# Moving four weight conversions from the second feed-forward layer into the first, in a fused attention and two-layer kernel

## The chip, the cores and the metric

The kernel runs on one core of one Trainium2 chip. The metric is the device time of one execution in microseconds. The kernel before was run three times on the clock alone, and once more with the profiler; the rows below come from that profiled execution.

## The reference

```python
def _attn_ref(q, k, v):                      # (2, 8, 576, 64), rotary positions
    q_rot, k_rot = (rotate(q), rotate(k))
    scores = np.matmul(q_rot, k_rot.transpose(0, 1, 3, 2)) / np.sqrt(D)
    attn = np.exp(scores - np.max(scores, axis=-1, keepdims=True))
    attn = attn / (np.sum(attn, axis=-1, keepdims=True) + 1e-09)
    return np.matmul(attn, v)

def _moe_ref(x, w_in, w_out):                # x (1152, 512), w_in (512, 2048), w_out (2048, 512)
    h = x @ w_in
    g = np.where(h > 0.0, h, np.exp(np.minimum(h, 0.0)) - 1.0)
    return g @ w_out

def _moe2_ref(x, w_in, w_out):               # same shapes, weights of its own
    h = x @ w_in
    return (h * np.tanh(softplus(h))) @ w_out
```

The attention result, laid out as 1152 tokens by 512 features, goes through the first layer and then through the second. The four weight arrays arrive as 64-bit floats.

## The kernel before

Every product is made from high and low parts of its operands: a value is kept as a rounded high part and the remainder, and three matrix products (high with high, low with high, high with low) are added up. XH and XL are the two parts of a layer's input, wi and wo followed by h or l those of its weights (a digit 0 or 1 tells even from odd groups, which have buffers of their own), g and ge those of the activated hidden values.

**The steps.** The 2048 hidden features are cut into 16 slices of 128, four slices make a group (GF = 4), and the tokens into two halves b of 576. A step is one slice for one half: 32 steps for the first layer, n = 0 to 31, and 32 for the second, n = 32 to 63; `half` in the code is 32. In each step TensorE runs `g1_mm` (24 matmuls, L183) into one of two PSUM buffers ps_s. In the first layer ScalarE (ACT) and VectorE (DVE) then make the ELU: L214, L215 and L216 on ACT, L217 and L218 on DVE (L218 is the last reader of ps_s), L223 on ACT (the high part) and L227 on DVE (the low part). When a group is complete for a half, four second products are due (`g2_first`, 24 matmuls, L619), one in each of the next four steps; DVE adds their result to Y at L629. For the last group of a half, L632 adds, L633 on ACT makes XH of the second layer and L634 on DVE makes XL. In the second layer L575 and L576 on ACT read ps_s, L577, L590 and L597 on DVE and L583, L589 and L596 on ACT follow, and `g2_second` (L648) multiplies with the output weights into ps_h. The steps 32 to 35 use the first four slices of the second layer, 36 to 39 the next four.

**The weight jobs.** One slice of one weight array is one job, 64 in all, in the order of the list `jobs`. A job loads the raw 64-bit words (SP queue, three buffers raw) and turns them into a 32-bit float wu (two buffers) and then into its two parts. It is opened with L96 on GpSimd (POOL) and goes on in four parts: a is L100, b is L104 and c is L108, all on DVE; d is L122 on ACT (the high part) and then L123 on POOL (the low part). `weight_part` does one part of the oldest open job, and two jobs are open at a time. Jobs 40 to 43 are the output weights wo0 of the second layer's first group, which its first `g2_second` needs.

**What sets the order.** In the first layer every engine's instructions stand in the order in which the code writes them. In a step from 4 to 30 there are three parts ahead of the ELU's first half and one part between its two halves, so each step does one job. From step 31 on, each step ends with one whole job, step 36 with two. In the second layer only ACT keeps the written order; a scheduler orders the others.

Of the kernel before, what the change touches and what calls it, by code (L numbers as in the profile page):

```python
# [27 lines left out]
def kernel(  # L28
# [22 lines left out]
    GF = 4  # L51
# [98 lines left out]
    def weight_part():  # L150
        while len(running) < 2 and opened[0] < len(jobs):
            open_job()
        if running:
            advance(0)

    def weight_job():
        n = min(njob[0] + 1, len(jobs))
        while njob[0] < n:
            weight_part()
# [15 lines left out]
    def g1_mm(m, f, b):  # L175
        c = m * NF + f
        hi, lo = WI[c]
        o = ps_s()
        k = 0
        for cc in range(NC):  # L180
            for w, x in ((hi, XH), (hi, XL), (lo, XH)):
                for j in range(2):
                    nc.tensor.matmul(  # L183
                        o[:, j, :HS], lhsT=w[:, cc, :], rhs=x[:, b, cc, j * HS:j * HS + HS],
                        start=(k == 0), stop=(k == 3 * NC - 1),
                    )
                k += 1
        return o
# [22 lines left out]
    def elu(m, f, b, o):  # L211
        h = o[:, :, :HS]
        t, g = tmp("ta"), tmp("tb")
        nc.scalar.activation(out=v2(g), in_=h, func=AF.Relu, scale=-1.0)  # L214
        nc.scalar.activation(out=t, in_=g, func=AF.Exp, scale=-1.0)  # L215
        nc.scalar.activation(out=g, in_=g, func=AF.Tanh, scale=-0.5)  # L216
        nc.vector.scalar_tensor_tensor(out=g, in0=t, scalar=1.0, in1=g, op0=ALU.add, op1=ALU.mult)  # L217
        nc.vector.tensor_tensor(out=v2(g), in0=v2(g), in1=h, op=ALU.max)  # L218
        return m, f, b, g

    def elu_hi(m, f, b, g):
        gh, gl = galloc(m, f, b)
        nc.scalar.activation(out=gh, in_=g, func=AF.Copy)  # L223
        return g, gh, gl

    def elu_lo(g, gh, gl):
        nc.vector.tensor_tensor(out=gl, in0=g, in1=plain(gh), op=ALU.subtract)  # L227
# [329 lines left out]
    def moe(mp, early):  # L557
# [15 lines left out]
        def mish_a(n, m, f, b, o):  # L573
            t, s = tmp("ta"), tmp("tb")
            nc.scalar.activation(out=v2(t), in_=o[:, :, :HS], func=AF.Tanh, scale=0.5)  # L575
            nc.scalar.activation(out=v2(s), in_=o[:, :, :HS], func=AF.Silu)  # L576
            nc.vector.scalar_tensor_tensor(out=s, in0=t, scalar=-3.0, in1=s, op0=ALU.add, op1=ALU.mult)  # L577
            mst[n] = (m, f, b, t, s)

        def mish_b(ns):  # L580
            for n in ns:
                t = mst[n][3]
                nc.scalar.activation(out=t, in_=t, func=AF.Ln, scale=-NEAR_HALF, bias=half_col)  # L583

        def mish_c(ns):
            nc.scalar.preload_act_table_set("silu_and_others")
            for n in ns:
                m, f, b, t, s = mst[n]
                nc.scalar.activation(out=t, in_=t, func=AF.Tanh, scale=-1.0)  # L589
                nc.vector.scalar_tensor_tensor(out=s, in0=t, scalar=1.0, in1=s, op0=ALU.add, op1=ALU.mult)  # L590

        def mish_d(ns):
            for n in ns:
                m, f, b, t, s = mst.pop(n)
                gh, gl = galloc(m, f, b)
                nc.scalar.activation(out=gh, in_=s, func=AF.Copy, scale=-0.25)  # L596
                nc.vector.scalar_tensor_tensor(  # L597
                    out=gl, in0=s, scalar=-0.25, in1=plain(gh), op0=ALU.mult, op1=ALU.subtract
                )
                seam(m, f, b)  # L600
# [60 lines left out]
        blocks[-4:] = [(1, g, b) for g in range(NG - 2, NG) for b in range(NB)]  # L661
        g1_seq = [(m, g * GF + fi, b) for m, g, b in blocks for fi in range(GF)]
        half = len(g1_seq) // 2
        D1, D2, LATE, XJ = 1, 4, (3, 4, 5, 7), 4
        pend = []

        def run_g2(it):
            if it[0] == 0:
                g2_first(*it[1])
            else:  # L670
                g2_second(*it[1])
# [6 lines left out]
        def step(n, late):  # L678
            m, f, b = g1_seq[n]
            o = early.pop(n) if n in early else g1_mm(m, f, b)  # L680
            if late:
                mish_c(late)
            done, late = late, []
            if m == 0:
                for _ in range(3 if GF <= n < half - 1 else 0):
                    weight_part()
                if o is not None:
                    o = elu(m, f, b, o)
                if GF <= n < half - 1:
                    weight_part()  # L690
                if o is not None:
                    o = elu_hi(*o)
            else:
                mish_a(n, m, f, b, o)
                mish_d(done)
            if f % GF == GF - 1:
                g = f // GF
                if m == 0:
                    pend.extend((n + (D1 if n < half - 1 else LATE[e]), (0, (g, b, e))) for e in range(NC))
                else:  # L700
                    pend.extend((n + D2, (1, (g, t))) for t in TB[b])
            if n in batches:
                late = batches[n]
                mish_b(late)
            cnt = 2 if len(pend) > 5 or pend and pend[0][1][0] == 0 and n in (half - 2, half + 6) else 1
            while pend and cnt and pend[0][0] <= n:
                run_g2(pend.pop(0)[1])
                cnt -= 1
            if m == 0:
                if o is not None:  # L710
                    elu_lo(*o)
            for _ in range(0 if n < half - 1 else 1 + (n == half + XJ)):
                weight_job()
            return late

# [9 lines left out]
        with tc.manual_schedule():  # L725
            while njob[0] < 2 * GF:
                weight_job()
            for n in range(half):
                step(n, [])
        with tc.manual_schedule(engines=MANUAL):  # L730
            late = []
            for n in range(half, 2 * half):
                if n == half + 7:
                    psum("ps_h")
                    s_more[0] = g_pool[0]
                    s_count[0] = 0
                late = step(n, late)
            mish_c(late)
            mish_d(late)
            while pend:  # L740
                run_g2(pend.pop(0)[1])
# [19 lines left out]
    with tc.tile_pool(name="mp", bufs=1, reuse_waits="tile") as mp:  # L761
        moe(mp, early)
# [54 lines left out]
```

## Time and profile before

| what | value |
|---|---|
| runs on the clock alone | 607.88, 608.4, 611.34 us; median 608.4 us |
| the profiled execution's own time | 612.44 us |
| its span, first to last instruction | 610.7 us |
| TensorE busy | 581.3 us (95%) |
| VectorE, ScalarE, GpSimd busy | 451.3, 372.4, 255.0 us |
| mean granted TensorE clock | 0.974 of full speed |

Busy shares are means over the attention (to about 200 us), the first layer (to about 385 us) and the second. What a stage is worth is read from its own stretch and from what its engines wait for.

### The profile page before, as it was taken

To read this page: it belongs to the slowest core of one execution; us is meant where nothing else is said; L and a number is where in the kernel's file an instruction comes from. 1 tells how busy PE (TensorE), PEld (TensorE's weight loads), DVE (VectorE), ACT (ScalarE), POOL (GpSimd) and SP (SyncE) were. 2 spreads that over 40 slices of the span, in tenths; PEclk is the share of its full clock that TensorE was granted. 3 is DMA by queue.
4 is the path that set the end of the run, shared out by engine and by line. 5 is a ranking of instruction groups with operands and counts; after the bars stand their busy time and mean duration, and the time that the engine had idled before them with its cause. 6 is when DMAs were issued, how large, how long until landed. Compare 5 with 4: busy or idle time off the path is not lost.

```text
span 610.7 us, 10253 instructions
## 1 busy us (share of the span) xinstructions
PE 581.3 (95%) x3794; PEld 503.7 (82%) x3794; DVE 451.3 (74%) x681; ACT 372.4 (61%) x637; POOL 255.0 (42%) x226
## 2 busy tenths in 40 slices
PE   6799999988899999999999999997899999999997
PEld 6676656655568999999999999996699998989985
DVE  5888998999972676677777778798588677674552
ACT  3357676765874665654545555793867868378660
POOL 5596685667780133232232332355243433532000
PEclk8779999998999999999999999999799999999999
DMA  6483577844530122232221322233332432300022
GB/s 215 128 234 115 115 195 196 240 105 126 163 99 0 35 101 75 70 104 70 84 91 69 104 70 75 68 124 99 103 90 83 138 87 70 121 18 1 17 85 89
DMA packets 43921, 62.17 MB, mean 102 GB/s; under 512 B 13920, under 2 KB 32096, under 8 KB 43104
## 3 DMA queue, kind: packets, MB, share of 16 engines
q1 hardware_dynamic: 43872, 61.52, 34.0%
q8 instruction: 30, 0.49, 0.3%
q14 instruction: 19, 0.16, 0.1%
HBM read 46.20 MB, written 2.36 MB: 80 GB/s over the span
## 4 chain that ended last, share of the span: by engine, by line
PE 36%; issue 28%; DVE 19%; POOL 13%; ACT 1%; DMA 1%; SPq 0%; POOLq 0%; ACTq 0%; DVEq 0%
PE ps_h L648 16%; PE ps_s L183 13%; DVE P L397 6%; DVE mn L373 5%; POOL wu L96 4%; PE ps_s L366 3%; POOL wi1l L123 3%; POOL wo0l L123 2%; PE psT L405 2%; PE psA L426 2%; POOL wo1l L123 2%; POOL wi0l L123 2%; DVE rc L390 2%; DVE wu L104 2%; DVE wu L100 1%
## 5 line engine op out<-in xcount | busy, mean ns | idle before, releaser
L380 ACT ACTIVATE P<-ps_s,mn 128x576 f32<-128x576 f32 x72 | 53.4, 741 | 39.1 <-DVE mn L373 30.7
L123 POOL TENSOR_TENSOR wi1l<-wu,wi1h 128x512 fp32r<-128x512 f32 x16 | 25.2, 1577 | 91.7 <-ACT wi1h L122 91.7
L373 DVE TENSOR_REDUCE mn<-ps_s 128x1 f32<-128x576 f32 x72 | 53.9, 748 | 11.4 <-PE ps_s L366 11.3
L405 PE MATMUL psT<-idn,P 128*128 128x128 f32 (+1 forms) x360 | 55.0, 286 | 6.5 <-DVE P L397 3.2
L417 ACT ACTIVATE pt<-psT 128x640 f32<-128x640 f32 x64 | 44.9, 702 | 23.9 <-PE psT L405 23.2
L100 DVE TENSOR_SCALAR wu<-wu 128x512 int32<-128x512 int32 x64 | 32.9, 514 | 34.0 <-POOL wu L96 34.0
L183 PE MATMUL ps_s<-XH,wi1h 128*128 128x288 f32 x256 | 55.1, 296 | 1.5 <-ACT tb L576 1.5
L183 PE MATMUL ps_s<-XH,wi0h 128*128 128x288 f32 x256 | 55.2, 297 | 0.9 <-DVE tb L218 0.8
L397 DVE TENSOR_SCALAR P<-P,rc 128x576 f32<-128x576 f32 x56 | 54.3, 970 | 1.0
L183 PE MATMUL ps_s<-XH,wi1l 128*128 128x288 f32 x256 | 54.8, 295 | 0.0
L183 PE MATMUL ps_s<-XL,wi1h 128*128 128x288 f32 x256 | 54.8, 295 | 0.0
L183 PE MATMUL ps_s<-XL,wi0h 128*128 128x288 f32 x256 | 54.7, 295 | 0.0
L183 PE MATMUL ps_s<-XH,wi0l 128*128 128x288 f32 x256 | 54.6, 295 | 0.0
L426 PE MATMUL psA<-pt,v_t 128*64 128x256 f32 (+1 forms) x320 | 54.5, 433 | 0.0
L104 DVE SCALAR_TENSOR_TENSOR wu<-raw,wu 128x512 int32<-128x512 int32 x64 | 51.1, 798 | 1.9
L108 DVE SCALAR_TENSOR_TENSOR wu<-raw,wu 128x512 int32<-128x512 int32 x64 | 50.6, 790 | 1.7
L405 PEld LDWEIGHTS psT<-idn,P 128*128 128x128 f32 (+1 forms) x360 | 40.7, 140 | 12.1 <-issue 3.7
L123 POOL TENSOR_TENSOR wo1l<-wu,wo1h 128x512 fp32r<-128x512 f32 x16 | 24.1, 1508 | 62.5 <-ACT wo1h L122 62.5
L96 POOL TENSOR_SCALAR wu<-raw 128x512 f32<-128x512 f32 x64 | 47.5, 743 | 5.1
L217 DVE SCALAR_TENSOR_TENSOR tb<-ta,tb 128x576 f32<-128x576 f32 x30 | 22.7, 758 | 34.1 <-ACT tb L216 33.8
L214 ACT ACTIVATE tb<-ps_s 128x576 f32<-128x576 f32 x30 | 19.6, 652 | 43.3 <-PE ps_s L183 43.3
L575 ACT ACTIVATE ta<-ps_s 128x576 f32<-128x576 f32 x32 | 20.6, 644 | 40.3 <-PE ps_s L183 40.3
(138 smaller groups left out, 1546.7 us busy)
## 6 DMA issues: line engine op xcount, KB each, us to landing
raw<-in_w_in_dram SPq DMA_DIRECT2D x32, 512.0 KB, 3.7
raw<-in_w_out_dram SPq DMA_DIRECT2D x32, 512.0 KB, 3.3
qk_t<-in_qk_dram SPq DMA_DIRECT2D x6, 1152.0 KB, 6.9
qa<-qh SPq DMA_DIRECT2D x28, 144.0 KB, 5.6
v_t<-in_vp_dram SPq DMA_DIRECT2D x8, 320.0 KB, 3.6
out_dram<-Y SPq DMA_DIRECT2D x9, 256.0 KB, 2.0
ka<-kh SPq DMA_DIRECT2D x14, 144.0 KB, 6.1
ka<-kl SPq DMA_DIRECT2D x14, 144.0 KB, 5.8
```

The costliest lines, as they stand in the source:

```text
L96: nc.gpsimd.tensor_scalar(out=u, in0=high.bitcast(F32), scalar1=REBASE, scalar2=0.0, op0=ALU.mult, op1=ALU.add)
L104: nc.vector.scalar_tensor_tensor(out=ui, in0=high, scalar=-0x80000000, in1=ui, op0=ALU.bitwise_and, op1=ALU.bitwise_or)
L108: nc.vector.scalar_tensor_tensor(out=ui, in0=low, scalar=29, in1=ui, op0=ALU.logical_shift_right, op1=ALU.bitwise_or)
L123: nc.gpsimd.tensor_tensor(out=lo, in0=u, in1=plain(hi), op=ALU.subtract)
L183: nc.tensor.matmul(o[:, j, :HS], lhsT=w[:, cc, :], rhs=x[:, b, cc, j * HS:j * HS + HS], start=(k == 0), stop=(k == 3 * NC - 1),)
L373: nc.vector.tensor_reduce(out=m, in_=psS[u][:, :, :HS], axis=AX.XY, op=ALU.min)
L380: nc.scalar.activation(out=P.rearrange("p (j n) -> p j n", j=2), in_=psS.pop(u)[:, :, :HS], func=AF.Exp, scale=-1.0, bias=mn_t.pop(u), acc ...
L397: eng.tensor_scalar(out=P, in0=P, scalar1=r, scalar2=None, op0=ALU.mult)
L405: nc.tensor.transpose(tv[:w, c, :], P[:, c * 128:c * 128 + w], idn)
L417: nc.scalar.activation(out=o, in_=tv, func=AF.Copy)
L426: nc.tensor.matmul(o[64 * h:64 * h + 64, :n], lhsT=v_t[p][:, c, 64 * h:64 * h + 64], rhs=pt_t[p, g][:, h, c, :], start=(c == 0), stop=(c = ...
L648: nc.tensor.matmul(o, lhsT=l, rhs=w, start=(k == 0), stop=(k == 3 * GF - 1))
```

## The change

```diff
-        D1, D2, LATE, XJ = 1, 4, (3, 4, 5, 7), 4
+        D1, D2, LATE = 1, 4, (3, 4, 5, 7)
+        AHEAD = half - 1 - 4 * GF
@@ in step(n, late)
-                for _ in range(3 if GF <= n < half - 1 else 0):
+                for _ in range((4 if n >= AHEAD else 3) if GF <= n < half - 1 else 0):
                     weight_part()
                 if o is not None:
                     o = elu(m, f, b, o)
@@ at the end of step
-            for _ in range(0 if n < half - 1 else 1 + (n == half + XJ)):
+            for _ in range(0 if n < half - 1 or half + 4 <= n < half + 7 else 1):
                 weight_job()
```

AHEAD is 15. In steps 15 to 30 five parts are done in place of four: four ahead of the ELU's first half and one between the halves. The 16 extra parts are four jobs, so job 39 instead of 35 is the next to finish when step 31 begins. In the second layer steps 36 to 38 finish no job, where steps 36, 37 and 38 finished two, one and one before; from step 39 on the two kernels are in phase again. No instruction is added or taken away.

A job takes four parts and a step now does five, so the place of the parts turns with a period of four steps (15 to 18, 19 to 22, 23 to 26, 27 to 30): `abcd|a`, `bcda|b`, `cdab|c`, `dabc|d`, the bar standing for the ELU's first half.

On ScalarE, the end of step 14, step 15 and most of step 16 (L122 is part d). Before:

```order
L223 ACTIVATE g<-tb 128x576
L214 ACTIVATE tb<-ps_s 128x576
L215 ACTIVATE ta<-tb 128x576
L216 ACTIVATE tb<-tb 128x576
L122 ACTIVATE wi0h<-wu 128x512
L223 ACTIVATE g<-tb 128x576
```

and with the change:

```order
L223 ACTIVATE g<-tb 128x576
L122 ACTIVATE wi0h<-wu 128x512
L214 ACTIVATE tb<-ps_s 128x576
L215 ACTIVATE ta<-tb 128x576
L216 ACTIVATE tb<-tb 128x576
L223 ACTIVATE g<-tb 128x576
L122 ACTIVATE wo0h<-wu 128x512
```

Part d stood behind L216 and now stands in front of L214; in every fourth step (`dabc|d`) a second one stands behind L216 as well.

On VectorE, from the last instruction of step 15 to the end of step 16. Before:

```order
L227 TENSOR_TENSOR g<-tb,g 128x576
L100 TENSOR_SCALAR wu<-wu 128x512
L104 SCALAR_TENSOR_TENSOR wu<-raw,wu 128x512
L108 SCALAR_TENSOR_TENSOR wu<-raw,wu 128x512
L217 SCALAR_TENSOR_TENSOR tb<-ta,tb 128x576
L218 TENSOR_TENSOR tb<-tb,ps_s 128x576
L629 TENSOR_TENSOR Y<-Y,ps_g 128x576
```

and with the change:

```order
L227 TENSOR_TENSOR g<-tb,g 128x576
L104 SCALAR_TENSOR_TENSOR wu<-raw,wu 128x512
L108 SCALAR_TENSOR_TENSOR wu<-raw,wu 128x512
L100 TENSOR_SCALAR wu<-wu 128x512
L217 SCALAR_TENSOR_TENSOR tb<-ta,tb 128x576
L218 TENSOR_TENSOR tb<-tb,ps_s 128x576
L104 SCALAR_TENSOR_TENSOR wu<-raw,wu 128x512
L629 TENSOR_TENSOR Y<-Y,ps_g 128x576
```

Part c, L108, which the L122 in front of this step's L214 waits for, still comes behind the L227 of the step before, and a fourth part stands between L218 and L629.

On ScalarE, from the last conversion of step 36 to step 38 (L575 and L576 read ps_s of a step; L633 writes XH). Before:

```order
L633 ACTIVATE XH<-Y 128x576
L122 ACTIVATE wo0h<-wu 128x512 x2
L575 ACTIVATE ta<-ps_s 128x576
L576 ACTIVATE tb<-ps_s 128x576
L122 ACTIVATE wo0h<-wu 128x512
L575 ACTIVATE ta<-ps_s 128x576
L576 ACTIVATE tb<-ps_s 128x576
L633 ACTIVATE XH<-Y 128x576
L122 ACTIVATE wo0h<-wu 128x512
```

and with the change:

```order
L633 ACTIVATE XH<-Y 128x576
L575 ACTIVATE ta<-ps_s 128x576
L576 ACTIVATE tb<-ps_s 128x576
L575 ACTIVATE ta<-ps_s 128x576
L576 ACTIVATE tb<-ps_s 128x576
L633 ACTIVATE XH<-Y 128x576
```

All four conversions to wo0h have left this place; they now stand between steps 31 and 36, where conversions to wi1h and wi0h stood, as many as before.

## Rows read from the trace of the kernel before

**Rows 1.** Busy time by stretch: length, then each engine's us, clock, DMA share, GB/s.

```profile
290.00:380.00 90.00, 90.00 (x680) 90.00 (x679) 68.56 (x102) 47.01 (x73) 27.85 (x28) 1.00 0.27 83
...
417.67:436.13 18.46, 12.04 (x50) 9.24 (x50) 13.05 (x17) 10.08 (x16) 8.26 (x8) 0.82 0.41 128
436.13:582.00 145.87, 145.87 (x876) 132.59 (x875) 99.99 (x146) 104.15 (x161) 48.14 (x38) 1.00 0.23 68
```

**Rows 2.** Timeline of TensorE, steps 38 to 41: start, us, instruction, [idle before it <-releaser].

```profile
417.25 0.42 PE L619 MATMUL ps_g<-g,wo1l 128*128 128x288 f32 x2
419.16 0.54 PE L183 MATMUL ps_s<-XH,wi1h 128*128 128x288 f32 x2 [1.49 <-ACT tb L576]
...
429.26 1.22 PE L648 MATMUL ps_h<-wo0h,g 128*128 128x512 f32 x2 [4.00 <-ACT wo0h L122]
...
436.13 0.43 PE L183 MATMUL ps_s<-XH,wi0h 128*128 128x288 f32 x2
...
439.31 0.63 PE L648 MATMUL ps_h<-wo0h,g 128*128 128x512 f32 x2
...
444.91 0.42 PE L183 MATMUL ps_s<-XH,wi0h 128*128 128x288 f32 x2
```

**Rows 3.** Timelines of DVE and ACT: part c, its part d and what follows.

```profile
421.86 0.69 DVE L108 SCALAR_TENSOR_TENSOR wu<-raw,wu 128x512 int32<-128x512 int32 x1
...
422.59 0.63 ACT L122 ACTIVATE wo0h<-wu 128x512 fp32r<-128x512 f32 x1 [3.48 <-DVE wu L108]
423.12 0.64 ACT L575 ACTIVATE ta<-ps_s 128x576 f32<-128x576 f32 x1
```

**Rows 4.** Timeline of step 25 from the end of its L183 matmuls, all engines.

```profile
340.35 0.69 PE L619 MATMUL ps_g<-g,wo0h 128*128 128x288 f32 x4
340.55 0.65 ACT L214 ACTIVATE tb<-ps_s 128x576 f32<-128x576 f32 x1 [1.94 <-PE ps_s L183]
341.24 0.69 ACT L215 ACTIVATE ta<-tb 128x576 f32<-128x576 f32 x1
341.95 0.69 ACT L216 ACTIVATE tb<-tb 128x576 f32<-128x576 f32 x1
342.67 0.76 DVE L217 SCALAR_TENSOR_TENSOR tb<-ta,tb 128x576 f32<-128x576 f32 x1 [1.35 <-ACT tb L216]
343.53 0.75 DVE L218 TENSOR_TENSOR tb<-tb,ps_s 128x576 f32<-128x576 f32 x1
344.20 0.75 DVE L629 TENSOR_TENSOR Y<-Y,ps_g 128x576 f32<-128x576 f32 x1
345.04 0.89 DVE L227 TENSOR_TENSOR g<-tb,g 128x576 fp32r<-128x576 f32 x1
345.86 0.42 DVE L100 TENSOR_SCALAR wu<-wu 128x512 int32<-128x512 int32 x1
346.31 0.69 DVE L104 SCALAR_TENSOR_TENSOR wu<-raw,wu 128x512 int32<-128x512 int32 x1
346.95 0.65 ACT L214 ACTIVATE tb<-ps_s 128x576 f32<-128x576 f32 x1 [1.94 <-PE ps_s L183]
347.03 0.69 DVE L108 SCALAR_TENSOR_TENSOR wu<-raw,wu 128x512 int32<-128x512 int32 x1
```

**Rows 5.** Timelines of DVE, ACT and PE: the last XL, and the start of step 32.

```profile
379.68 0.75 DVE L632 TENSOR_TENSOR Y<-Y,ps_g 128x576 f32<-128x576 f32 x1
...
380.46 0.68 ACT L633 ACTIVATE XH<-Y 128x576 fp32r<-128x576 f32 x1 [2.85 <-DVE Y L632]
...
381.18 0.76 DVE L634 TENSOR_TENSOR XL<-Y,XH 128x576 fp32r<-128x576 f32 x1 [0.75 <-ACT XH L633]
...
381.86 0.43 PE L183 MATMUL ps_s<-XH,wi0h 128*128 128x288 f32 x2
```

**Rows 6.** Timelines of POOL and DVE: a DVE part while POOL runs L123.

```profile
423.30 1.40 POOL L123 TENSOR_TENSOR wo0l<-wu,wo0h 128x512 fp32r<-128x512 f32 x1 [2.02 <-ACT wo0h L122]
...
423.47 1.78 DVE L104 SCALAR_TENSOR_TENSOR wu<-raw,wu 128x512 int32<-128x512 int32 x1
```

## The prediction

> **What bounds the kernel now.** I read the busy times by stretch first, to see where TensorE is not the bound. In the second half of the first layer it is busy 90.00 of 90.00 us at full clock while VectorE has 21 us to spare, and from 436 to 582 us it is again busy without a gap; between them stands one hole, 12.04 busy of 18.46 us at a granted clock of 0.82, a mean of its two levels of 1.2 and 2.4 GHz [rows 1]. Then TensorE's timeline in that hole. Step 39 waits 1.49 us for L576 to free ps_s, and the first second-layer product L648 waits 4.00 us for a high part of its output weights, jobs 40 to 43; what follows the long wait runs stretched, since the clock fell [rows 2]. Then, for the cause, ScalarE and VectorE: L122 waits for part c on VectorE, 3.48 us in one place, and L575 of the next step stands right behind it [rows 3]. So the conversions arrive late, and where they stand in ScalarE's queue they also hold up the release of ps_s. Last, the timeline of one regular step, to see what the first layer has to spare [rows 4].
>
> **What the change removes.** The four wo0 conversions leave steps 36 to 38. Without them L575 and L576 of step 37 stand directly behind L633, and the weights that L648 needs are there. From the end of L619 at 417.67 (417.25 + 0.42) to the start of step 40 at 436.13 TensorE takes 18.46 us. The work in it is 24 matmuls L183 and 24 L648, which without waits take 439.31 - 436.13 = 3.18 and 444.91 - 439.31 = 5.60 us [rows 2], 8.78 in sum. If nothing else is late, 9.7 us go. The loads on the SP queue move forward with their jobs; each is issued three jobs before use and the period of a job stays above 5 us, so I cost them at nothing.
>
> **What the change adds.** The extra parts look free, a quarter of a job per step, 0.42 + 0.69 + 0.69 = 1.80 us of VectorE in four, so 0.45 us against some 1.5 us that VectorE idles in a step of 6.40 us (21.4 of 90 us [rows 1]). But their place matters more than their size. Before, d stood behind L216, and VectorE could do a, b and c while ScalarE ran L214 to L216. Now a d stands in front of every L214. In three steps of four it waits for a c that VectorE reaches only behind the L227 of the step before. That closes a loop from VectorE over ScalarE back to VectorE, once a step, with no engine able to run ahead.
>
> I add up the loop from start to start. From c over d to L214: 422.59 - 421.86 = 0.73 and 423.12 - 422.59 = 0.53 [rows 3]. L214 to L215 0.69, to L216 0.71, to L217 0.72, to L218 0.86 [rows 4]. From c to L218 that is 4.24. On VectorE an instruction that waits for nothing follows after 0.08 less than the duration of the one ahead (L218 of 0.75 to L629: 0.67), a to b takes 0.45 and b to c 0.72 [rows 4]. From one L227 to the next:
> - step 15, abcd|a: 0.67 + 0.45 + 0.72 + 4.24 + 0.67 + 0.34 + 0.67 = 7.76
> - step 16, bcda|b: 0.67 + 0.72 + 4.24 + 0.67 + 0.61 + 0.67 = 7.58
> - step 17, cdab|c: 0.67 + 4.24 + 0.67 + 0.61 + 0.67 = 6.86
> - step 18, dabc|d, where the first d has its c from the step before: 0.67 + 0.45 + 0.72 + 0.61 + 0.86, and from L218 to L227 1.51 as before, 4.82
>
> The four make 27.02 us where TensorE needs 4 x 6.40 = 25.60. VectorE falls behind by 1.42 us in every four steps, although it is never full.
>
> TensorE feels that late. L227 started 4.69 us after its matmuls had ended (345.04 - 340.35 [rows 4]); the second products need it only for their last slice, one step and most of a product later, at 6.40 + 20/24 of 3.2 less the 0.8 of L227 itself, some 8.3 us after, so 3.6 us are to spare. Counting back eleven steps from step 25, L227 of step 14 starts at 345.04 - 11 x 6.40 = 274.64. Three cycles and one long step later, in step 27, it starts at 274.64 + 3 x 27.02 + 7.76 = 363.46. In steps 28 to 30 L632, L633 and L634 come into the loop: from L632 to L634 1.50 us (381.18 - 379.68 [rows 5]), since L634 waits for ScalarE. Step 28 takes 7.58 + 1.50 and step 29 6.86 + 1.50, which gives 380.90. In step 30, 3.31 us to L218 (0.67 + 0.45 + 0.72 + 0.61 + 0.86), then L632, a, b, L634 and the second L632 (0.67 + 0.67 + 0.45 + 0.61 + 0.67) and 1.50 to the last L634: 388.78. Before, it started at 381.18 [rows 5]: 7.6 us later. Step 32 needs this last XL at its end, 381.86 + 3.2 = 385.06, and had it at 381.94; so 3.1 of the 7.6 are slack and TensorE is 4.5 us late. These 4.5 us are the lower bound of this term unless the loop does not act at all.
>
> **What VectorE and GpSimd cost each other.** L104 took 1.78 us beside an L123, against 0.69 alone [rows 4, 6]: it stood still for most of the subtraction. Before, L123 fell into the time of L218 and L629, which read PSUM, and hardly met anything. With the parts turning, I find three meetings in a cycle when I lay the GpSimd queue beside the loop (an L96 in front of L227 in dabc|d, the delayed L123 in front of L217 in the next step, an L96 in front of L217 in cdab|c), which hold VectorE 0.24, 0.53 and 0.21 us: 0.98 in sum. The bounds are 0 and three whole meetings of 1.09 (1.78 - 0.69), 3.3 us a cycle. I take 0.75, nearer to the lower end because the step of rows 4 has an L227 of 0.89, a meeting that cost only some 0.14 us. There are some three and a half cycles up to the seam, so this adds 2.6 us.
>
> The Trainium skill (SBUF — State Buffer, section "SBUF: two separate sides") says that VectorE and GpSimd hold their shared port pair as an exclusive lock for a whole instruction, so that the later one blocks fully. The L104 of 1.78 us agrees. By that rule taken at its worst, three meetings with whole subtractions of some 1.3 us would cost 3.9 us a cycle and turn the sum into a loss; the sum here goes by the partial meetings.
>
> **The sum.** 9.7 gained, 4.5 + 2.6 = 7.1 lost: 2.6 us faster, in the profiled execution 612.44 to 609.8. That execution lies 4.0 us above the median of the runs, 608.4. The edits change a stretch in the middle and nothing that would depend on that offset, so the median becomes 605.8.
>
> **The rivals.**
> First, the lag does not reach TensorE: the whole gain stands, 608.4 - 9.7 = 598.7. For it: VectorE's idle time, 1.5 us a step, exceeds the 0.45 us added, and TensorE waited for nothing in this stretch. Against it: the loop adds up from rows, without any estimate, to more than the period.
> Second, slower than before: the meetings of VectorE and GpSimd lengthen the loop until the loss is above 9.7. From 4.5 on that takes 5.2 us, or 1.5 us a cycle, about one full L123 each. At the bound of 3.3 us a cycle the loss is 4.5 + 11.6 = 16.1, and the time 608.4 + 6.4 = 614.8. For it: VectorE did stand still beside L123 [rows 6]. Against it: in most of the loop VectorE's instructions follow each other closely, and then it is GpSimd that waits. (The rule of the Trainium skill on the port pair, above, leads to this rival.) TensorE's new waits could also let the granted clock fall, as the 4 us wait did [rows 2]; most of such a stretch would lie inside the next wait for the loop, so only the last one, at the seam, would count.
> Third, the change does not bring wo0 forward in time: the conversions keep their places in ScalarE's dense run and arrive with the same lag. The order speaks against it, since all four stand ahead of L575 of step 36. Then only the loss would be left, 608.4 + 7.1 = 615.5.
>
> **How the numbers follow.** The forecast, both halves at work with meetings of 0 to 1.4 us a cycle, 598.7 + 4.5 = 603.2 to 608.4, gets 0.58, with its point at 605.8; the first rival 0.18; the second 0.19; the third and anything else 0.05. A measurement of this kernel can tell about 1% from no change, 6.1 us, so faster means below 602.3 and slower above 614.5. Faster is the first rival and a tail of the forecast, 0.20; slower the far part of the second and third, 0.07; the rest, 0.73, is within. The range goes from 599.5, which takes in part of the first rival, to 611, which takes in the near half of the second.
>
> **What the profile after would show.** Right: the waits of L648 for wo0h and wo0l and of step 39 for L576 are gone, the stretch from the last L619 to step 40 takes about 9 us at full clock, and TensorE shows new waits in the first layer, first in second products of steps 24 and 28 for L227 and then around steps 30 to 32 for L632, L218 or L634; L122 on ScalarE waits for L108 in three steps of four, and L227 in step 27 starts 10 us or more after its matmuls end. Wrong: TensorE runs through to step 32 without a wait (first rival), or the waits ahead of step 32 exceed 9.7 us (second), or L648 still waits for wo0 (third).

## The result: slower by 1.3 per cent

| | median, us | runs | ratio to before, 95% interval |
|---|---|---|---|
| before, in the same session | 609.87 | 607.88 to 611.72 (4) | |
| with the change | 617.64 | 616.75 to 618.65 (4) | 1.0128 [1.0085, 1.0172] |

The prediction was 605.8 us with a range up to 611.0, so it was wrong: the kernel became slower where it was to become faster. The result is near the second rival, meetings of 1.5 us a cycle and more (up to 614.8), and beyond it.

**The hole is gone.** TensorE's timeline of the changed kernel, steps 38 to 40, answers to [rows 2]:

```profile
432.19 0.43 PE L619 MATMUL ps_g<-g,wo1l 128*128 128x288 f32 x2
...
435.66 0.63 PE L648 MATMUL ps_h<-wo0h,g 128*128 128x512 f32 x2
...
441.25 0.42 PE L183 MATMUL ps_s<-XH,wi0h 128*128 128x288 f32 x2
```

From 432.62 to 441.25 are 8.63 us where there were 18.46, and no wait stands in them. The busy times by stretch, laid over the same places, answer to [rows 1]:

```profile
290.00:380.00 90.00, 85.65 (x615) 84.13 (x614) 66.74 (x98) 41.83 (x66) 31.01 (x30) 0.96 0.29 88
380.00:420.00 40.00, 36.08 (x264) 34.91 (x263) 34.18 (x46) 27.74 (x42) 16.45 (x14) 1.00 0.34 109
...
432.61:441.25 8.64, 8.64 (x50) 7.56 (x48) 2.27 (x3) 5.99 (x9) 0.00 (x0) 1.00 0.01 3
```

The stretch of the hole is full at full clock, but from 290 to 380 us TensorE is no longer busy all the time (85.65 of 90), while VectorE is busy less, not more (66.74 against 68.56). No engine has become full. TensorE's timeline tells what it waits for there (the wait and its releaser stand in brackets):

```profile
310.57 0.53 PE L619 MATMUL ps_g<-ge,wo0h 128*128 128x288 f32 x2 [0.61 <-ACT ge L223]
...
311.52 0.54 PE L619 MATMUL ps_g<-ge,wo0h 128*128 128x288 f32 x2 [0.42 <-DVE ge L227]
...
339.63 1.80 PE L619 MATMUL ps_g<-g,wo0h 128*128 128x288 f32 x4 [2.55 <-ACT g L223]
...
385.06 0.79 PE L619 MATMUL ps_g<-g,wo1h 128*128 128x288 f32 x4 [1.86 <-DVE Y L632]
...
392.20 0.50 PE L183 MATMUL ps_s<-XH,wi0h 128*128 128x288 f32 x2 [0.49 <-DVE tb L218]
...
395.29 0.53 PE L183 MATMUL ps_s<-XL,wi0h 128*128 128x288 f32 x2 [0.99 <-DVE XL L634]
...
426.10 0.53 PE L183 MATMUL ps_s<-XH,wi1h 128*128 128x288 f32 x2 [2.39 <-ACT tb L576]
```

These are the kinds of waits that the prediction named, in second products and then for L632, L218 and L634, but they begin a cycle earlier, in steps 20 and 24 where 24 and 28 were named, since the lag grows by 3.4 us a cycle (29.0 against 25.6, below). L227 of step 27 starts 9.1 us after its matmuls end (368.82 and 359.69), where 10 or more were named, for TensorE itself was late by then. After the wait of 2.55 us the four matmuls take 1.80 us, where four take 0.69 in [rows 4]: the granted clock is 0.50 from 339.60 to 345.00, its level of 1.2 GHz, and 1.00 again from 355 us on. L227 keeps its cycle of 29.04 us across this stretch (339.78 to 368.82), so the next wait for the loop takes it up, as the prediction said; at the seam the clock stays at 1.00 (the row from 380 us).

**The loop.** Start times of L227 on VectorE from step 14 on: 273.88, 281.77, 289.32, 296.29, 302.54, then 310.72, 318.33, 325.30, 331.55 and so on to 368.82 in step 27. The steps are 7.89, 7.55, 6.97, 6.25 and later 8.2, 7.6, 6.97, 6.25; a full cycle takes 29.0 us. The sum of rows gave 7.76, 7.58, 6.86, 4.82, which is 27.02, and 27.77 with the 0.75 for meetings. Of the 2.0 us above the sum 1.43 lie in `dabc|d` (step 18), 0.45 in the `abcd|a` behind it, whose L227 ahead is stretched, and 0.1 in the other two. VectorE's timeline there, and GpSimd's:

```profile
296.29 0.75 DVE L227 TENSOR_TENSOR g<-tb,g 128x576 fp32r<-128x576 f32 x1
296.95 1.52 DVE L100 TENSOR_SCALAR wu<-wu 128x512 int32<-128x512 int32 x1
298.51 1.02 DVE L104 SCALAR_TENSOR_TENSOR wu<-raw,wu 128x512 int32<-128x512 int32 x1
299.57 0.69 DVE L108 SCALAR_TENSOR_TENSOR wu<-raw,wu 128x512 int32<-128x512 int32 x1
...
302.54 1.12 DVE L227 TENSOR_TENSOR ge<-tb,ge 128x576 fp32r<-128x576 f32 x1
```

```profile
296.45 1.74 POOL L123 TENSOR_TENSOR wo0l<-wu,wo0h 128x512 fp32r<-128x512 f32 x1 [2.82 <-ACT wo0h L122]
298.28 0.71 POOL L96 TENSOR_SCALAR wu<-raw 128x512 f32<-128x512 f32 x1
...
302.41 0.64 POOL L96 TENSOR_SCALAR wu<-raw 128x512 f32<-128x512 f32 x1
```

L100, alone 0.42, takes 1.52 because L123 has begun 0.50 us ahead of it; L104, alone 0.69, takes 1.02 behind L96; L227, alone 0.75, takes 1.12 behind the next L96. The first of these meetings is the dear one, and neither it nor the one of L104 was among the three that the prediction found.

### The profile page after: what moved, and what is told of

Read it like the earlier page. It is cut to its first block, busy times and chain, and to the rows that moved or that the text cites. A ratio compares the mean times of both kernels' runs of the same rounds, so it can differ in the third digit from the quotient of the medians.

```text
span 615.8 us, 10255 instructions
## 1 busy us (share of the span) xinstructions
PE 583.2 (95%) x3794; PEld 504.9 (82%) x3794; DVE 451.3 (73%) x681; ACT 372.0 (60%) x637; POOL 254.0 (41%) x226
## 4 chain that ended last, share of the span: by engine, by line
PE 53%; DVE 29%; ACT 9%; issue 5%; POOL 3%; DMA 1%; SPq 0%; DVEq 0%; ACTq 0%; POOLq 0%
PE ps_s L183 22%; PE ps_h L648 16%; PE ps_g L619 6%; DVE P L397 6%; DVE mn L373 5%; PE ps_s L366 3%; PE psA L426 3%; DVE wu L104 3%; DVE wu L108 3%; PE psT L405 3%; DVE tb L217 2%; DVE tb L218 2%; DVE wu L100 2%; ACT ta L215 2%; ACT tb L216 2%
## 5 line engine op out<-in xcount | busy, mean ns | idle before, releaser
L123 POOL TENSOR_TENSOR wi1l<-wu,wi1h 128x512 fp32r<-128x512 f32 x16 | 22.9, 1429 | 87.5 <-ACT wi1h L122 87.5
L183 PE MATMUL ps_s<-XH,wi1h 128*128 128x288 f32 x256 | 55.8, 300 | 2.8 <-ACT tb L576 2.8
L397 DVE TENSOR_SCALAR P<-P,rc 128x576 f32<-128x576 f32 x56 | 56.1, 1001 | 1.0
L183 PE MATMUL ps_s<-XH,wi0h 128*128 128x288 f32 x256 | 55.3, 298 | 1.5 <-DVE tb L218 1.3
L100 DVE TENSOR_SCALAR wu<-wu 128x512 int32<-128x512 int32 x64 | 34.4, 538 | 30.0 <-POOL wu L96 30.0
L183 PE MATMUL ps_s<-XL,wi0h 128*128 128x288 f32 x256 | 54.8, 295 | 1.0 <-DVE XL L634 1.0
L183 PE MATMUL ps_s<-XL,wi1h 128*128 128x288 f32 x256 | 55.6, 299 | 0.0
L183 PE MATMUL ps_s<-XH,wi1l 128*128 128x288 f32 x256 | 55.5, 298 | 0.0
L183 PE MATMUL ps_s<-XH,wi0l 128*128 128x288 f32 x256 | 54.6, 295 | 0.0
L123 POOL TENSOR_TENSOR wo1l<-wu,wo1h 128x512 fp32r<-128x512 f32 x16 | 24.3, 1521 | 72.3 <-ACT wo1h L122 72.3
L217 DVE SCALAR_TENSOR_TENSOR tb<-ta,tb 128x576 f32<-128x576 f32 x30 | 23.1, 769 | 41.3 <-ACT tb L216 41.3
L108 DVE SCALAR_TENSOR_TENSOR wu<-raw,wu 128x512 int32<-128x512 int32 x64 | 50.8, 794 | 1.4
L104 DVE SCALAR_TENSOR_TENSOR wu<-raw,wu 128x512 int32<-128x512 int32 x64 | 49.5, 774 | 1.7
L96 POOL TENSOR_SCALAR wu<-raw 128x512 f32<-128x512 f32 x64 | 48.4, 757 | 5.1
L575 ACT ACTIVATE ta<-ps_s 128x576 f32<-128x576 f32 x32 | 20.6, 645 | 42.5 <-PE ps_s L183 42.5
L183 PEld LDWEIGHTS ps_s<-XH,wi1h 128*128 128x128 f32 x256 | 42.4, 192 | 3.8 <-ACT tb L576 3.2
```

The lines of the kernel that those rows point to most:

```text
L96: nc.gpsimd.tensor_scalar(out=u, in0=high.bitcast(F32), scalar1=REBASE, scalar2=0.0, op0=ALU.mult, op1=ALU.add)
L100: nc.vector.tensor_scalar(out=ui, in0=ui, scalar1=3, scalar2=0x7FFFFFF8, op0=ALU.logical_shift_left, op1=ALU.bitwise_and)
L104: nc.vector.scalar_tensor_tensor(out=ui, in0=high, scalar=-0x80000000, in1=ui, op0=ALU.bitwise_and, op1=ALU.bitwise_or)
L108: nc.vector.scalar_tensor_tensor(out=ui, in0=low, scalar=29, in1=ui, op0=ALU.logical_shift_right, op1=ALU.bitwise_or)
L123: nc.gpsimd.tensor_tensor(out=lo, in0=u, in1=plain(hi), op=ALU.subtract)
L183: nc.tensor.matmul(o[:, j, :HS], lhsT=w[:, cc, :], rhs=x[:, b, cc, j * HS:j * HS + HS], start=(k == 0), stop=(k == 3 * NC - 1),)
```

## The experiments

All were run in two groups of four, each group beside 15 runs of the kernel before (medians 610.26 and 611.73 us). The ratios to it are those on record, with their 95% intervals; they differ a little from the quotients of these medians.

### Whole jobs in place of turning parts

The same four jobs ahead and the same pause, but each extra job stands undivided at the end of steps 15, 19, 23 and 27. So the part d of every step keeps its place behind L216, and only every fourth L214 has a d, that of the extra job, in front of it. The edit is shown against the changed kernel.

```diff
...
-                for _ in range((4 if n >= AHEAD else 3) if GF <= n < half - 1 else 0):
+                for _ in range(3 if GF <= n < half - 1 else 0):
...
-            for _ in range(0 if n < half - 1 or half + 4 <= n < half + 7 else 1):
+            for _ in range(int(n >= AHEAD and n % GF == GF - 1) if n < half - 1 else int(not half + 4 <= n < half + 7)):
```

> The same four jobs are done ahead, but as one whole job at the end of steps 15, 19, 23 and 27, so that the parts keep their old places and only every fourth L214 has an extra d in front of it. Loop theory (a d in front of L214 whose c comes behind the L227 of the step before makes the chain from VectorE over ScalarE and back longer than the period): the one late step in four starts L214 about 1.2 us late and VectorE's idle 1.5 us per step takes that back, so TensorE waits for nothing in the first layer, the hole ahead of step 40 is about 8.7 us, and the time is some 9.7 us below the kernel before, ratio 0.984. Work theory (the extra conversions themselves, their VectorE time and their meetings with GpSimd, are too much for the first layer): the same 20 jobs in the same 16 steps, so the lag at step 32 stays near 11 us and the time near that of the changed kernel, ratio 1.01.

Measured: 601.8 us (600.24 to 602.21), ratio 0.9848 [0.9823, 0.9874]. From 202 to 480 us this is TensorE's only wait:

```profile
384.94 0.54 PE L183 MATMUL ps_s<-XH,wi0h 128*128 128x288 f32 x2 [0.73 <-DVE tb L218]
```

VectorE does the same work as in the changed kernel. L227 of step 16 comes 8.20 us after that of step 15 (279.75 to 287.95), but the next only 4.98 later: without a d in front of the next L214 the lag is made good at once. The same work costs TensorE one wait of 0.73 us here; it is its order that costs. This version beats both kernels.

### The changed kernel with part d behind L216

Where a part d would stand in front of L214, it now stands behind L216; all else is as in the change. `running[0][1]` counts how far the oldest job is, and at 4 its part d is next.

```diff
...
+    def front_parts(k):
+        held = 0
+        for _ in range(k):
...
+            if not held and running[0][1] == 4:
+                held = 1
+            else:
+                advance(held)
+        return held
...
-                for _ in range((4 if n >= AHEAD else 3) if GF <= n < half - 1 else 0):
-                    weight_part()
+                held = front_parts((4 if n >= AHEAD else 3) if GF <= n < half - 1 else 0)
...
+                if held:
+                    advance(0)
                 if GF <= n < half - 1:
                     weight_part()
```

> The changed kernel with one thing undone: a part d that would stand in front of L214 is put behind L216, where it stood before; the five parts per step, their VectorE order and the jobs moved ahead stay. Loop theory: TensorE runs through to step 32 without waits of more than some tenths, the gain of about 9.7 us remains, ratio to the kernel before about 0.984. Work theory: VectorE does the same parts at the same rate and the lag stays, ratio 1.01.

Measured: 603.93 us (603.59 to 604.07), ratio 0.9887 [0.986, 0.9915]. L227 comes every 25.5 us in four steps (273.01, 298.52, 324.00, 349.58), which is TensorE's 4 x 6.40. One place in ScalarE's order, and with it the time at which GpSimd's L123 and L96 come behind d, makes the difference of 13.7 us to the changed kernel. The meetings with GpSimd remain (L100 takes 1.51 us at 299.34 and L104 1.02 at 300.89), and without the loop only a little of them reaches TensorE: a wait of 1.50 us for L218 in step 33, where waits of some tenths and a ratio of 0.984 were expected.

### All four parts in front, nothing ahead

The kernel before with part d in front of the ELU in every step, at the same number of jobs.

```diff
-                for _ in range(3 if GF <= n < half - 1 else 0):
+                for _ in range(4 if GF <= n < half - 1 else 0):
                     weight_part()
...
-                if GF <= n < half - 1:
-                    weight_part()
```

> The kernel before, no job moved ahead, with all four parts of a step's job in front of the ELU's first half, so that d stands in front of L214 in every step from 4 to 30. Loop theory: from L227 to L227 0.67 + 0.45 + 0.72 + 4.24 + 1.51 = 7.59 us where TensorE needs 6.40, over 27 steps some 32 us less 3.6 us of slack, so about 635 to 640 us. Work theory: the amount of work per step is the same as before, so the time stays near 609 us.

Measured, one run: 648.63 us. From L227 to L227 are 7.59 us, as summed, in step after step (266.49, 274.08, 281.66, 289.25, 296.84). Not an instruction more than in the kernel before, and 38 us longer: the loop is shown by itself. The time is some 10 us above what was expected. L218 of step 31 starts 38.5 us later than in the kernel before (421.32 against 385.04, with the attention 2.2 us shorter), so all of the loss has arisen by the seam; which term of the expected sum was too small is open.

### GpSimd without its reads, in two steps

The changed kernel, in the 20 jobs of steps 15 to 30. First L123's subtraction becomes a memset to zero, which leaves out the low parts of these weights; then L96, which in the first of the two runs still reads (other than its expectation says), becomes a memset to a constant as well, which leaves out their values.

```diff
-        nc.gpsimd.tensor_tensor(out=lo, in0=u, in1=plain(hi), op=ALU.subtract)
+        if 19 <= jobs.index(key) < 39:
+            nc.gpsimd.memset(plain(lo), 0.0)
+        else:
+            nc.gpsimd.tensor_tensor(out=lo, in0=u, in1=plain(hi), op=ALU.subtract)
```

and in the second run besides

```diff
+            if 19 <= jobs.index(key) < 39:
+                nc.gpsimd.memset(u, REBASE)
+            else:
+                nc.gpsimd.tensor_scalar(
...
```

> The changed kernel, but the 20 jobs of steps 15 to 30 set the low part of their weights to zero with a memset in place of the subtraction L123, so GpSimd reads no SBUF there; part of the weights' precision is left out. If the meetings of L123 with VectorE's parts lengthened the cycle of four steps from 27.0 to the 29.0 us that were measured, the cycle falls to between 27.0 and 27.5 us, the lag at step 32 from 11 to about 5 to 6 us, and the time to about 611 us. If the meetings are not the cause (another cost that my sum left out), the cycle stays at 29 us and the time at 617 us.

> The changed kernel, where in the 20 jobs of steps 15 to 30 GpSimd reads nothing: L123's subtraction writes zeros and L96's scaling writes a constant. It leaves out the low parts and the values of these weights. The kernel without the subtraction alone had a cycle of 28.07 us in four steps, against 29.04 in the changed kernel and 27.02 in the sum without meetings. Theory one, the rest of the cycle above the sum is L96's meetings with VectorE: the cycle falls to 27.0 to 27.3 us, about 1 us a cycle less, and the time by 3 to 4 us from 613.4 to about 610 (ratio 0.995 to 1.002). Theory two, the sum itself is too short by a microsecond (gaps between engines are longer than the rows gave): the cycle stays near 28 us and the time at 613.

Measured: 613.44 us, ratio 1.0051 [1.0031, 1.0071], without the subtraction; 611.68 us, 1.0011 [0.9991, 1.0031], without both. The cycle is 28.07 us (323.80 to 351.87) without L123 and 27.5 (308.96 to 336.49) without both, against 29.04. So of the 2.0 us above the sum the subtraction makes 1.0 and L96 0.55, each at least, since a memset stands in its place. Both expectations were half right: the first had given all of the 2.0 us to the subtraction, and in the second 0.5 us a cycle stay. Its first four steps are 7.76, 7.55, 6.83 and 5.15, later ones 7.82, 7.61, 6.88 and 5.22, beside the sums 7.76, 7.58, 6.86 and 4.82. Nearly all that is left lies again in `dabc|d`, and VectorE's and GpSimd's timelines show why (L103 is L100 there, L233 is L227, L97 and L127 are the memsets):

```profile
295.99 0.75 DVE L233 TENSOR_TENSOR g<-tb,g 128x576 fp32r<-128x576 f32 x1
296.66 0.75 DVE L103 TENSOR_SCALAR wu<-wu 128x512 int32<-128x512 int32 x1
```

```profile
296.13 0.53 POOL L97 MEMSET wu<- 128x512 f32 x1 [3.90 <-ACT wo0h L125]
296.60 0.53 POOL L127 MEMSET wo0l<- 128x512 f32 x1
```

Part a is held 0.33 us by a memset, which reads nothing, while L233 keeps its 0.75 and the other memset beside it its 0.53.

### TensorE's order at the seam

Behind step 32 TensorE's order had changed: a second product L619 now stands inside step 32 and ahead of step 33, and from the start of step 32 to the end of the last L619 40.4 us went by where there had been 35.8. I took this for a second cost of 4.6 us and put TensorE in the written order there, in the changed kernel and, for a control, in the one with whole jobs.

```diff
-        with tc.manual_schedule(engines=MANUAL):
+        with tc.manual_schedule(engines=MANUAL | {mybir.EngineType.PE}):
             late = []
-            for n in range(half, 2 * half):
+            for n in range(half, half + 7):
+                late = step(n, late)
+        with tc.manual_schedule(engines=MANUAL):
...
```

> The changed kernel, but in steps 32 to 38 TensorE keeps the order in which the code writes the products: the first slice of the late second product L619 then stands behind step 34 instead of inside step 32. It is close to the order of the kernel before, which had four of these 24 matmuls behind step 32. Between the start of step 32 and the end of the last L619 the kernel before took 35.8 us, the changed kernel 40.4. Theory one, the new order makes these 4.6 us (it holds up steps 33 and 34, and with them ScalarE's dense run): the stretch falls to 36 to 38 us, the wait of 2.39 us for L576 in step 38 goes, and the time falls by 2.5 to 4.5 us, from about 617.6 to 613 to 615 (ratio about 1.007 to the kernel before). Theory two, the lateness of the last XL makes them, whatever the order: the stretch stays at about 40 us and the time at 617 to 618 (ratio 1.012).

> The kernel with whole jobs (four jobs ahead, no turning of the parts), with the same written order on TensorE in steps 32 to 38: a control for the order by itself. If the order costs or gives nothing where nothing is late, it takes 601 to 602.5 us as the kernel with whole jobs did (ratio 0.984 to 0.987). If the written order saves or costs something of its own, it differs from that by more than 1 us, and the run with the same order in the changed kernel has to be read less that difference.

Measured: 619.42 us, ratio 1.0146 [1.0117, 1.0176], and for the control 603.85 us, 0.9888 [0.9859, 0.9917]. The written order costs some 2 us of its own where nothing is late (0.9888 against 0.9848, a difference about as large as the intervals of the two), and less those the changed kernel would take 617.0, as much as with its own order. So theory one fell: the time did not fall by 2.5 to 4.5 us, and the other order brings nothing back. What it does is to show the wait that the new order had covered, in step 33 of the first of the two:

```profile
399.47 0.85 PE L183 MATMUL ps_s<-XH,wi0h 128*128 128x288 f32 x2 [2.05 <-DVE tb L218]
```

Step 33 waits for L218 of step 31 to free ps_s. The same wait is the only one at the start of the seam with whole jobs (0.73 us) and with d behind (1.50 us).

### The pause in another place

Whole jobs as above, but the pause in steps 32 to 35, and two, one and one jobs in steps 36 to 38 as in the kernel before.

```diff
-            for _ in range(int(n >= AHEAD and n % GF == GF - 1) if n < half - 1 else int(not half + 4 <= n < half + 7)):
+            for _ in range(int(n >= AHEAD and n % GF == GF - 1) if n < half - 1 else 0 if half <= n < half + 4 else 1 + (n == half + 4)):
```

> The kernel with whole jobs, with the pause in another place: no job in steps 32 to 35, and in steps 36 to 38 two, one and one as in the kernel before, so that the four conversions to wo0 stand again where they stood, in ScalarE's run from step 36 to 38. All four jobs are still done ahead in the first layer. Theory one, the place of the wo0 conversions makes the hole: L648 waits for wo0h again, the stretch from the last L619 to step 40 is back at about 16 to 18.5 us, and the time is 601.8 + 7 to 10, so 609 to 612 (ratio 0.997 to 1.003). Theory two, the load of ScalarE ahead of it makes the hole, and four conversions fewer in steps 32 to 35 let the rest come in time: the stretch stays near 9 us and the time at 601 to 603 (ratio 0.986).

Measured: 605.67 us (603.14 to 607.72), ratio 0.9908 [0.9876, 0.9941]. TensorE's timeline in the place of the hole:

```profile
417.56 0.43 PE L619 MATMUL ps_g<-g,wo1l 128*128 128x288 f32 x2
...
424.46 0.74 PE L648 MATMUL ps_h<-wo0h,g 128*128 128x512 f32 x2 [1.16 <-ACT wo0h L122]
426.34 0.50 PE L648 MATMUL ps_h<-wo0l,g 128*128 128x512 f32 x1 [1.15 <-POOL wo0l L123]
...
429.47 0.43 PE L183 MATMUL ps_s<-XH,wi0h 128*128 128x288 f32 x2
```

From 417.99 to 429.47 are 11.48 us, neither the 8.6 of the other place nor 16 to 18.5. It is neither of the two theories. Most of the hole, 7.0 of 9.8 us, went with the number of conversions from the end of step 31 to step 38 (nine before, five here), and 2.8 go with their standing in steps 36 to 38.

## Why the prediction was wrong

The time of the profiled execution can be made up from the two traces. The attention took 1.00 us less this time (L227 of step 14 at 273.88 against 274.88), so 1.00 is added to times of the changed kernel below. Its last L619 ends at 433.62, before at 417.67: 15.95 lost. The hole then gives 9.83 back. That is 6.1 longer from there on, and 612.44 + 6.1 - 1.0 = 617.5; the profiled execution took 617.58.

**What the change removes** was right in its size, 9.83 for 9.7. Its reason was right in part: the prediction had the place of the wo0 conversions make the whole hole, and with these in their old place 7.0 of the 9.8 us still went.

**The loop** was right as a mechanism and, where GpSimd hardly interferes, in its numbers: L227 of step 15 comes after 7.76 us with the memsets, as summed, and L122 waited for L108 in three steps of four. The first rival (the lag does not reach TensorE) is out, and so is the third: with the loop taken out (d behind, whole jobs) the gain stands, and the stretch of the hole takes 8.64 us in both.

**The loss** was sized at 4.5 + 2.6 = 7.1 and is 15.95. Two steps failed.

First, the meetings of VectorE and GpSimd. The prediction took 0.75 us a cycle "because the step of rows 4 has an L227 of 0.89, a meeting that cost only some 0.14 us". They cost 2.0 in the cycle. The row was read without the other engine's row, GpSimd's:

```profile
344.67 0.66 POOL L96 TENSOR_SCALAR wu<-raw 128x512 f32<-128x512 f32 x1
```

This L96 ended at 345.33, so L227, begun at 345.04, met only its last 0.29 us. What a meeting costs is what is left of GpSimd's instruction, less some 0.14: L100 of step 18 ends 0.28 us after L123 does, L104 0.54 after its L96, L227 0.61 after its own, each about 0.14 less than it takes alone. Besides, of the three meetings that the prediction found, two took place, at L227 (0.37 for 0.24) and at L217 of `cdab|c` (0.14 for 0.21); the one of 0.53 did not. The two that it missed, L100 with 1.10 and L104 with 0.33, make most of the 1.94 us that the rows of one cycle give.

How late this made the last XL (L634): it starts at 381.18 in the kernel before; summed without meetings 7.6 later; measured 9.6 later without GpSimd's reads, 11.0 without L123 and 16.5 in the changed kernel. So 8.9 where 2.6 was allowed: 5.5 went with the subtraction, 1.4 with L96, and 2.0 stay without both. Of these 0.24 is the start of the sum (274.64, where the trace has 274.88), 1.3 the cycles with the memsets (0.33 to 0.40 in each `dabc|d`), and 0.46 an L96 of a later job that still reads, beside the L227 of step 29 (1.21 for 0.75 in that run).

The Trainium skill (SBUF — State Buffer, section "SBUF: two separate sides") had said that whichever of the two engines starts first gets the port pair for its whole instruction and the other blocks. The rows above agree: L123, begun 0.16 us behind L227, takes 1.74 for the 1.29 that it takes alone, and L100, begun behind L123, takes 1.52. The 3.9 us a cycle that I drew from it as the worst case was too high, but the mechanism was the rival that came true. Not every row agrees. In the second layer of the kernel before, an L123 has begun ahead of L634 and L108, and these two keep their own time while it takes 3.81:

```profile
402.51 3.81 POOL L123 TENSOR_TENSOR wi1l<-wu,wi1h 128x512 fp32r<-128x512 f32 x1 [3.71 <-ACT wi1h L122]
```

```profile
403.14 0.75 DVE L634 TENSOR_TENSOR XL<-Y,XH 128x576 fp32r<-128x576 f32 x1
403.81 0.68 DVE L108 SCALAR_TENSOR_TENSOR wu<-raw,wu 128x512 int32<-128x512 int32 x1
```

So the order in which two instructions begin does not settle every meeting. The section also names which VectorE instructions take part: those with two inputs in SBUF, which are in the way only of a GpSimd one that reads, and those in a two-port mode. L233 and the memset beside it, 0.75 and 0.53, agree with the first; part a with its one input, 0.75 in place of 0.42 beside a memset, was held as the second kind would be, though no trace here shows its mode.

Second, the slack. "So 3.1 of the 7.6 are slack and TensorE is 4.5 us late" counted the slack of step 32's last XL. But what comes next is L218 of step 31, which frees ps_s for step 33. In the kernel before, VectorE's and TensorE's timelines show it already without slack, 385.04 + 0.75 against a start at 385.85:

```profile
385.04 0.75 DVE L218 TENSOR_TENSOR tb<-tb,ps_s 128x576 f32<-128x576 f32 x1
```

```profile
385.85 0.54 PE L183 MATMUL ps_s<-XH,wi0h 128*128 128x288 f32 x2
```

No wait is seen there, since four matmuls of a second product stood between the steps and ended just then. In the changed kernel L218 ends at 400.25 and step 33 starts right behind it, 15.5 us later than before:

```profile
399.50 0.75 DVE L218 TENSOR_TENSOR tb<-tb,ps_s 128x576 f32<-128x576 f32 x1
```

```profile
400.35 0.50 PE L183 MATMUL ps_s<-XH,wi0h 128*128 128x288 f32 x2
```

How late the last XL, L218 of step 31 and the last L619 start, against the kernel before and with the attention's difference taken out, in us:

| kernel | last XL | L218, step 31 | last L619 |
|---|---|---|---|
| whole jobs | 1.6 | 0.6 | 0.7 |
| d behind | 2.8 | 1.8 | 3.2 |
| GpSimd without reads | 9.6 | 8.6 | 9.1 |
| without L123 | 11.0 | 10.0 | 11.9 |
| the change | 16.5 | 15.5 | 15.9 |
| the change, written order | 16.4 | 15.4 | 18.3 |

L218 is 1.0 less late than XL in each, and TensorE is late by at least what L218 is. So at step 33 the slack was 1.0 us where 3.1 had been counted, and by the last L619 another 0.5 of it was lost: 0.5 were left (16.5 less 15.95), and 2.6 of the 3.1 were not there. The 1.4 to 2.9 us that three of the kernels lose beyond L218 were not taken apart.

With both, 7.1 + (8.9 - 2.6) + 2.6 = 16.0, for 15.95 measured. That this closes proves little, since the 0.5 was taken from the 15.95; what stands by itself are the rows of the meetings and those of L218 and step 33.

## What to carry to other kernels

Before a piece of work is moved on an in-order queue, follow who waits for it and whom it waits for: if its input is made behind the last result of the round before, the two engines run one after the other, and time that an engine idles is of no use. A moved part keeps its price but may get a new place, so move whole units, or keep each part where it stood. And slack has to be counted for every consumer of a late engine, not for the first one that comes to mind: a zero wait in the trace may be a buffer freed just in time.

## What was not expected of the hardware

A GpSimd instruction with one input, L96, holds VectorE just as the subtraction with two does (L104 1.02 beside it for 0.69, L227 1.12 for 0.75), and even a memset holds part a (0.75 for 0.42), though not L233 (0.75). A late instruction on VectorE does not take its whole own time after the other's end, but some 0.14 us less (L100, L104 and L227 above). And a GpSimd instruction that has begun can still be passed by several VectorE instructions in a row (the L123 of 3.81).
